# Rotary attention and two feed-forward layers on one core: weight conversion every four units, rotation and stacks as separate steps

## The chip, the cores and the metric

The kernel runs on one core of a Trainium2 chip. The metric is the device time of one execution in microseconds (us); a figure for a kernel is the median of several runs.

## The reference

The input is q, k and v for 4 batches, 8 heads, 576 positions and 64 dimensions; the output of the attention goes through two feed-forward layers of width 512 to 2048 to 512.

```python
q_rot, k_rot = (rotate(q), rotate(k))
scores = scale * np.matmul(q_rot, k_rot.transpose(0, 1, 3, 2))
attn = np.exp(scores - np.max(scores, axis=-1, keepdims=True))
attn = attn / (np.sum(attn, axis=-1, keepdims=True) + 1e-09)
x = np.matmul(attn, v)                        # to 2304 tokens x 512
h = x @ w_in                                  # first layer
g = np.where(h >= 1, h, np.where(h <= -1, 0.0, (h + 1) ** 2 / 4))
x = g @ w_out
r = np.maximum(x @ w2_in, 0.0)                # second layer
out = (s * (r * r) + b) @ w2_out
```

All matrix products are made from two float32r parts of each operand (high and low), so that one product is three matmuls: high by high, high by low, low by high. The weights come as 64-bit floats and are split into the two parts on the chip.

## The kernel before

**Attention in units.** Two heads of one batch make a pair; there are 16 pairs of nine units, 144 units in all. A unit is one block of 128 queries of one head (unit 2 of a pair: the remaining 64 of both heads). `qk` (L314) makes its scores on TensorE, the negated row maximum on VectorE (L327) and the exponent on ScalarE (L330). Two units later `tmain` and `trem` (L333, L351) transpose the result on TensorE and split it into its parts (ScalarE L345, VectorE L349); four units later `av` (L364) multiplies by v. `finish_pair` (L399) divides by the sums and writes the pair to `xd` in device memory.

**What a pair needs beforehand.** `load_qk` and `load_v` fetch q, k and v through SyncE's DMA queue. `rope_pair` (L260) rotates q or k: a multiply and an add on POOL (`pool_tt`, L83, in pieces of 288 columns), the high part on ScalarE (L270, L273), the low part on VectorE for q (L271) and on POOL for k. `stack` (L280) copies the parts to their places for the score matmuls by DMAs in SyncE's queue: `qs` for q, `kh` (high part, twice) and `kz` (low part) for k. `v_pair` (L294) splits v on ScalarE and POOL. For pair i + 1 this is written into the units of pair i: q rotated at unit 1, k at 3, v loaded at 5 and split at 7.

**Weight halves.** The first layer's weights are 16 slices, of which 8 (`set_a`) are used beside the attention: group 0 is slices 0 to 3, group 1 slices 4 to 7. Each slice has two halves (one for h, one for y), and each half is made by six steps (L106): load (SyncE, L117), `bias` (ScalarE, L127), `shift` (VectorE, L132 and L133), `high` (ScalarE, L136), `rest` (VectorE, L141 and L142) and `low_part` (POOL, L146 and L147). The scratch tiles `wa` and `wm` have one buffer, the loaded `wraw` has two, so one half follows the other. `convert(n)` (L485) takes the next half from `pending` and sets its load for unit n and its steps for n + 2, n + 2, n + 3, n + 3 and n + 4.

**Pieces.** `beside` (L435) gives the first layer's work on chunks of 288 tokens and one weight group: four h pieces and four y pieces of 12 matmuls each, 80 pieces in all, for five of the eight chunks. They go into units with a budget (`run_fill`, L501): each unit adds its share, a piece costs 1. Batch 0 feeds 16 pieces of group 0 (from unit 39 at the earliest), batch 1 feeds 48 (from unit 75), batch 2 feeds 16 (from unit 111). A new chunk is loaded and split four units ahead (`split_x`).

**Order.** The loop at L568 writes for each unit: q (scores), l (loads and preparations of the next pair), t (transposes), a (value product), f (pieces). Steps that were set for a later unit with `put` are written by `run_later` right after q; `behind` (L224) makes each of their ScalarE and VectorE instructions stand behind the last exponent and the last maximum written so far. A scheduler then fixes one order for each engine's and each DMA queue's instructions, and every engine keeps it. In the attention it may move an instruction ahead of earlier written ones where nothing ties it; instructions that are not written through `behind` (the rotation, stacks and split of v) are not tied, nor are those on POOL and SyncE.

**After the attention** the `stage` function (L593) computes the rest of the first layer and the second layer in five stages, with the other 48 weight halves converted on the way.

Of the kernel before, what the change touches and what calls it, by code (L numbers as in the profile page):

```python
# [57 lines left out]
def kernel(ctx, tc, qq, kk, vv, tab, ww1, ww2, s, b, out):  # L58
# [162 lines left out]
    def put(n, fn, *args):  # L221
        later.setdefault(n, []).append((fn, args))
# [7 lines left out]
    def run_later(n):  # L230
        for fn, args in later.pop(n, []):
            behind(fn, *args)
# [24 lines left out]
        for j in range(2):  # L257
            nc.gpsimd.memset(kz_t[j][n][D:].bitcast(F32), 0.0)

    def rope_pair(i, nm, eng, lo_eng, pieces=WHOLE):  # L260

        t = qk_in.pop((nm, i))
        hi, lo = t[:, 0, :].bitcast(F32R), t[:, 1, :].bitcast(F32R)
        for c in pieces:
            tt = pool_tt if eng is nc.gpsimd else nc.vector.tensor_tensor
            tt(out=t[:, :, c], in0=t[:, :, c], in1=tab_sb[:, :, c], op=ALU.mult)
            r = t[:, 1, c]
            tt(out=r, in0=t[:, 0, c], in1=r, op=ALU.add)
            if nm == "q":
                nc.scalar.activation(hi[:, c], r, AF.Copy, scale=0.125)  # L270
                nc.vector.scalar_tensor_tensor(out=lo[:, c], in0=r, scalar=0.125, in1=t[:, 0, c], op0=ALU.mult, op1=ALU.subtract)  # L271
            else:
                nc.scalar.copy(hi[:, c], r)  # L273
                pool_tt(out=lo[:, c], in0=r, in1=t[:, 0, c], op=ALU.subtract)
        parts_t[nm, i] = t
        if i > 0:
            stack(i, nm, 0)
            stack(i, nm, 1)

    def stack(i, nm, j):  # L280
        t = parts_t[nm, i][j * D:(j + 1) * D]
        if nm == "q":
            st = stacks["q", i, j] = qs_t[j][i % 2]
            st = st[:, j * D:j * D + S].bitcast(F32)
            nc.sync.dma_start(out=st[:D], in_=t[:, 0, :])
            return nc.sync.dma_start(out=st[D:], in_=t[:, 1, :]).ins
        kh = att.tile([P, S], F32R, tag="kh", name="kh", bufs=4)
        kz = kz_t[j][i % 2]
        stacks["k", i, j] = kh, kz
        nc.sync.dma_start(out=kh[:D].bitcast(F32), in_=t[:, 0, :])  # L290
        nc.sync.dma_start(out=kh[D:].bitcast(F32), in_=t[:, 0, :])
        return nc.sync.dma_start(out=kz[:D].bitcast(F32), in_=t[:, 1, :]).ins

    def v_pair(i):  # L294
        t = v_in[i]
        vs = att2.tile([P, 5, 4, D], F32R, tag="vs", name="vs")
        nc.scalar.copy(vs[:, :, 0::3, :], t)
        pool_tt(out=vs[:, :, 1:3, :], in0=t, in1=vs[:, :, 0::3, :], op=ALU.subtract, dim=1)
        vs_t[i] = vs

# [127 lines left out]
    def split_x(c, n):  # L428

        put(n, x_load, c)  # L430
        for k in range(KD):
            put(n + 2 + k // 2, x_split, k)
        return n + 4

    def beside(work):  # L435
        ready = split_x(work[0][0], max(now + 2, 45))
        for n, (c, gi) in enumerate(work):
            while now < ready:
                yield None
# [26 lines left out]
            load_qk(0, "k", HALVES)  # L466
    load_qk(0, "q", HALVES)
    load_v(0)
    rope_pair(0, "k", nc.vector, nc.gpsimd, HALVES)
    rope_pair(0, "q", nc.vector, nc.vector, HALVES)  # L470
    for j in range(2):
        stack(0, "k", j)
        first = stack(0, "q", j)
    v_pair(0)
    nc.sync.dma_start(out=s_sb, in_=s.to_broadcast([P, 1]))
    nc.sync.dma_start(out=b_sb, in_=b.to_broadcast([P, 1]))
    load_qk(1, "q")
# [22 lines left out]

    def run_fill(budget):  # L501
        nonlocal done
        done = min(done, 1.0)
        done += budget
        while fill and done > 0:
            try:
                cost = next(fill[0])
                if cost is None:
                    break
                done -= cost  # L510
            except StopIteration:
                fill.pop(0)
        if not fill:
            done = 0.0
# [9 lines left out]
    def do_load(n):  # L524
        if n < len(units):
            i, k = units[n]
            if i + 1 < NPAIR:
                if k == 0:
                    load_qk(i + 1, "k")
                elif k == 1:  # L530
                    rope_pair(i + 1, "q", nc.gpsimd, nc.vector)
                elif k == 3:
                    rope_pair(i + 1, "k", nc.gpsimd, nc.gpsimd)
                elif k == 5:
                    load_v(i + 1)
                elif k == 7:
                    v_pair(i + 1)
                    if i + 2 < NPAIR:
                        load_qk(i + 2, "q")

        if n in range(31, 49, 2) or n in range(70, 110, 4):
            convert(n + 1)

    def do_t(n):
        if LT <= n < len(units) + LT:
# [15 lines left out]
                    fill.append(beside(ORDERS[i // NP]))  # L561

    def do_fill(n):
        run_fill(0.0 if n < 48 else 0.85 if n < 90 else 0.98)

    acts = {"q": do_qk, "l": do_load, "t": do_t, "a": do_av, "f": do_fill}
    now = 0
    while now < len(units) + LA or fill or later:  # L568
        with ExitStack() as st:
            if now < 36:  # L570
                st.enter_context(tc.issue_after(first))
            for o in ORDER:
                acts[o](now) if now < len(units) + LA or o == "f" else None
                if o == "q":
                    run_later(now)
        now += 1
    pa.close()
    pp.close()
# [148 lines left out]
```

## Time and profile before

| | us |
|---|---|
| median of 3 runs | 1209.62 (1208.05 to 1211.63) |
| the profiled execution | 1214.03 |
| its span, first to last instruction | 1212.20 |

| | PE | VectorE (DVE) | ScalarE (ACT) | POOL |
|---|---|---|---|---|
| busy, us | 1117.4 | 789.8 | 605.1 | 608.2 |
| share of the span | 92% | 65% | 50% | 50% |

The share of a whole span mixes stages with different limits, so the argument cuts the span into stretches. PE is TensorE's matmuls, PEld its weight loads, SPq the DMA queue of SyncE. A busy PE is counted with the overlap of neighbouring matmuls, so it can be busy without being at its peak. "A <- B" in a list of waits means that A stood idle until B was done. The mean granted clock of TensorE was 0.975 of full speed.

### The profile page before, as it was taken

What the parts mean: (1) busy time and instruction counts of PE and PEld (TensorE: products, weight loads), DVE (VectorE), ACT (ScalarE), POOL (GpSimd) and SP (SyncE); (2) the same over time, 40 slices, a digit from 0 to 9 for tenths busy, and PEclk for the clock granted to TensorE, in tenths of its full rate; (3) what the DMA queues carried; (4) which work ended last, traced back from release to release, by engine and by line L of the source; (5) the groups of instructions that cost most, each with busy time, mean ns of one, the idle gap of its engine ahead of it and who ended that gap; (6) DMA issues with size and microseconds to landing.
All of it is one profiled execution on the core that took longest, in us unless ns stands there. A gap on an engine that the chain in (4) does not pass through costs nothing.

```text
span 1212.2 us, 19147 instructions
## 1 busy us (share of the span) xinstructions
PE 1117.4 (92%) x6628; PEld 1034.4 (85%) x6628; DVE 789.8 (65%) x1363; ACT 605.1 (50%) x1319; POOL 608.2 (50%) x782
## 2 busy tenths in 40 slices
PE   3898875988899999999989999999999999999998
PEld 3687764988899998999989999999888889988887
DVE  4589985789887777587766667777763333434443
ACT  3688753677677766555444443444443233222221
POOL 6778787278765401366668988566541101110100
PEclk9899877899999999999999989999999999999999
DMA  8775653365465420343335545443421101312210
GB/s 228 197 199 164 193 151 120 92 196 172 146 188 148 118 75 18 100 132 120 122 93 149 165 146 159 125 131 96 154 64 63 32 32 63 93 33 64 71 62 34
DMA packets 76033, 142.69 MB, mean 118 GB/s; under 512 B 11680, under 2 KB 49568, under 8 KB 75936
## 3 DMA queue, kind: packets, MB, share of 16 engines
q1 hardware_dynamic: 75936, 141.47, 39.5%
q8 instruction: 52, 0.85, 0.3%
q14 instruction: 45, 0.37, 0.1%
HBM read 91.29 MB, written 26.54 MB: 97 GB/s over the span
## 4 chain that ended last, share of the span: by engine, by line
PE 48%; DVE 18%; POOL 14%; issue 8%; ACT 7%; DMA 5%; SPq 1%; POOLq 0%; ACTq 0%; DVEq 0%
PE hps L154 14%; PE yps L640 5%; PE yps L642 5%; PE yps L641 5%; POOL w L83 5%; PE y L154 4%; POOL wm L83 4%; PE av L154 4%; PE sc L154 4%; PE h L154 3%; POOL xl L83 3%; PE tp L343 2%; DVE nm L327 2%; DVE wm L133 2%; ACT wa L127 2%
## 5 line engine op out<-in xcount | busy, mean ns | idle before, releaser
L154 PE MATMUL hps<-xh,w 128*128 128x464 f32 (+5 forms) x1216 | 346.6, 350 | 3.5 <-POOL w L83 2.5
L154 PEld LDWEIGHTS hps<-xh,w 128*128 128x128 f32 x1216 | 223.2, 189 | 19.1 <-POOL w L83 2.8
L640 PE MATMUL yps<-gh,w 128*128 128x464 f32 (+5 forms) x608 | 214.1, 352 | 6.8 <-ACT yo L647 5.9
L83 POOL TENSOR_TENSOR xl<-xs,xh 128x232 fp32r<-128x232 f32 (+5 forms) x140 | 107.4, 796 | 215.3 <-ACT xh L87 215.2
L641 PE MATMUL yps<-gl,w 128*128 128x464 f32 (+5 forms) x608 | 213.0, 350 | 2.5 <-DVE gl L91 2.5
L642 PE MATMUL yps<-gh,w 128*128 128x464 f32 (+5 forms) x608 | 212.5, 350 | 0.0
L154 PE MATMUL hps<-xl,w 128*128 128x464 f32 (+5 forms) x608 | 212.4, 349 | 0.0
L83 POOL TENSOR_TENSOR wm<-wm,w 128x256 f32<-128x256 f32 x128 | 114.0, 910 | 135.6 <-DVE wa L141 70.1
L327 DVE TENSOR_REDUCE nm<-sc 128x1 f32<-128x576 f32 x144 | 108.1, 751 | 47.6 <-PE sc L154 46.3
L184 DVE TENSOR_TENSOR ar<-ar,hps 128x464 f32<-128x464 f32 (+1 forms) x80 | 50.5, 632 | 132.7 <-ACT ar L183 132.7
L154 PE MATMUL sc<-kh,qs 128*128 128x288 f32 x320 | 102.3, 335 | 35.3 <-DMA qs<-qin 16.8
L640 PEld LDWEIGHTS yps<-gh,w 128*128 128x128 f32 x608 | 114.7, 189 | 18.1 <-ACT yo L647 9.2
L641 PEld LDWEIGHTS yps<-gl,w 128*128 128x128 f32 x608 | 114.9, 189 | 11.1 <-DVE gl L91 3.6
L154 PEld LDWEIGHTS hps<-xl,w 128*128 128x128 f32 x608 | 115.0, 189 | 7.6
L642 PEld LDWEIGHTS yps<-gh,w 128*128 128x128 f32 x608 | 114.8, 189 | 7.5
L330 ACT ACTIVATE p<-sc,nm 128x576 f32<-128x576 f32 x144 | 107.0, 744 | 15.0 <-DVE nm L327 10.4
L183 ACT ACTIVATE ar<-hps 128x464 f32<-128x464 f32 (+1 forms) x80 | 44.1, 553 | 124.4 <-PE hps L154 124.2
L349 DVE TENSOR_TENSOR ptl<-tp,pth 128x512 fp32r<-128x512 f32 x134 | 90.4, 682 | 22.4 <-ACT pth L345 21.8
L154 PEld LDWEIGHTS sc<-kh,qs 128*128 128x128 f32 x320 | 63.9, 200 | 45.0 <-ACT p L330 23.2
L345 ACT CAST pth<-tp 128x512 fp32r<-128x512 f32 x134 | 78.1, 586 | 46.0 <-PE tp L343 45.0
L83 POOL TENSOR_TENSOR w<-wm,wa 128x256 fp32r<-128x256 f32 x128 | 99.3, 794 | 1.4 <-DVE wa L142 1.4
L154 PE MATMUL y<-gh,w 128*128 128x288 f32 x320 | 78.1, 313 | 20.0 <-POOL w L83 11.0
(87 smaller groups left out, 2340.0 us busy)
## 6 DMA issues: line engine op xcount, KB each, us to landing
wraw<-in_ww SPq DMA_DIRECT2D x64, 512.0 KB, 3.8
kh<-kin SPq DMA_DIRECT2D x64, 144.0 KB, 2.6
qs<-qin SPq DMA_DIRECT2D x64, 144.0 KB, 2.6
qin<-in_q SPq DMA_DIRECT2D x15, 576.0 KB, 4.8
kin<-in_k SPq DMA_DIRECT2D x15, 576.0 KB, 3.9
xs<-y1d SPq DMA_DIRECT2D x32, 232.0 KB, 2.5
yd<-ys SPq DMA_DIRECT2D x40, 144.0 KB, 2.1
vin<-in_v SPq DMA_DIRECT2D x16, 320.0 KB, 3.8
```

Of the source, the lines that this page charges most:

```text
L83: nc.gpsimd.tensor_tensor(out=out[c], in0=in0[c], in1=in1[c], op=op)
L127: nc.scalar.activation(t["a"], top, AF.Copy, scale=2.0 ** -112)
L154: nc.tensor.matmul(out_ps, l, r, start=(i == 0), stop=(i == n - 1))
L183: nc.scalar.activation(r, ps, AF.Relu)
L184: nc.vector.tensor_tensor(out=r, in0=r, in1=ps, op=ALU.mult)
L327: anchors["DVE"] = nc.vector.tensor_reduce(out=nm, in_=sc[:, :, :288], axis=AX.XY, op=ALU.max, negate=True).ins
L330: anchors["ACT"] = nc.scalar.activation(p, sc[:, :, :288], AF.Exp, bias=nm, scale=1.0, accum_out=sums_t[i][:, col:col + 1]).ins
L345: nc.scalar.copy(hi, v)
L349: nc.vector.tensor_tensor(out=lo, in0=v, in1=hi, op=ALU.subtract)
L640: nc.tensor.matmul(acc, wh, gh, start=f == 0, stop=False)
L641: nc.tensor.matmul(acc, wh, gl, start=False, stop=False)
L642: nc.tensor.matmul(acc, wl, gh, start=False, stop=last)
```

## The change

- Halves: `convert` is called at units 16, 20, ..., 44 and 64, 68, ..., 92, for that unit itself. Before it was at 31, 33, ..., 47 and 70, 74, ..., 106 for the next unit (16 halves in all in both).
- Pieces: the budget starts at unit 44 (48 before) with 0.6 a unit up to 71 and 0.98 from there (0.85 up to 89, then 0.98), and up to 2.0 of it may be saved (1.0 before). The first chunk is set for now + 2; the bound "not before unit 45" is gone.
- `rope_pair`, `stack` and `v_pair` become single steps, set with `put` for the units shown below; so their ScalarE and VectorE instructions stand behind that unit's maximum and exponent. The first pair (`rope_first`) stays as it was, apart from the order of its stack DMAs.
- Loads: k of the pair after next at unit 8 and its q at unit 6 (k of the next pair at 0, q of the pair after next at 7 before); v at 2 (5 before).
- `run_later` moves from behind q to the end of the unit.

```diff
-    def rope_pair(i, nm, eng, lo_eng, pieces=WHOLE):
...
+    def rope_mult(i, nm):
+        t = parts_t[nm, i] = qk_in.pop((nm, i))
+        pool_tt(out=t, in0=t, in1=tab_sb, op=ALU.mult)
+
+    def rope_add(i, nm):
+        t = parts_t[nm, i]
+        pool_tt(out=t[:, 1, :], in0=t[:, 0, :], in1=t[:, 1, :], op=ALU.add)
+
+    def rope_hi(i, nm):
...
+    def rope_lo(i, nm):
...
+    def stack_q(i):
...
+    def stack_k(i):
+        for j in range(2):
+            t = parts_t["k", i][j * D:(j + 1) * D]
+            kh = att.tile([P, S], F32R, tag="kh", name="kh", bufs=4)
+            stacks["k", i, j] = kh, kz_t[j][i % 2]
+            nc.sync.dma_start(out=kh[:D].bitcast(F32), in_=t[:, 0, :])
+            nc.sync.dma_start(out=kh[D:].bitcast(F32), in_=t[:, 0, :])
+
+    def stack_z(i):
+        for j in range(2):
+            t = parts_t["k", i][j * D:(j + 1) * D]
+            nc.sync.dma_start(out=kz_t[j][i % 2][:D].bitcast(F32), in_=t[:, 1, :])
...
-        ready = split_x(work[0][0], max(now + 2, 45))
+        ready = split_x(work[0][0], now + 2)
...
-        done = min(done, 1.0)
+        done = min(done, 2.0)
...
                 if k == 0:
-                    load_qk(i + 1, "k")
-                elif k == 1:
-                    rope_pair(i + 1, "q", nc.gpsimd, nc.vector)
-                elif k == 3:
-                    rope_pair(i + 1, "k", nc.gpsimd, nc.gpsimd)
-                elif k == 5:
-                    load_v(i + 1)
-                elif k == 7:
-                    v_pair(i + 1)
-                    if i + 2 < NPAIR:
-                        load_qk(i + 2, "q")
-
-        if n in range(31, 49, 2) or n in range(70, 110, 4):
-            convert(n + 1)
+                    if i == 0:
+                        load_qk(1, "k")
+                    for dn, fn, nm in ((0, rope_mult, "q"), (1, rope_add, "q"), (2, rope_hi, "q"), (3, rope_lo, "q"),
+                                       (2, rope_mult, "k"), (3, rope_add, "k"), (4, rope_hi, "k"), (5, rope_lo, "k")):
+                        put(n + dn, fn, i + 1, nm)
+                    put(n + 2, load_v, i + 1)
+                    put(n + 4, stack_q, i + 1)
+                    put(n + 5, stack_k, i + 1)
+                    put(n + 6, stack_z, i + 1)
+                    put(n + 5, v_hi, i + 1)
+                    put(n + 6, v_lo, i + 1)
+                if k == 6 and i + 2 < NPAIR:
+                    load_qk(i + 2, "q")
+                if k == 8 and i + 2 < NPAIR:
+                    load_qk(i + 2, "k")
+
+        if n in range(16, 48, 4) or n in range(64, 96, 4):
+            convert(n)
...
-        run_fill(0.0 if n < 48 else 0.85 if n < 90 else 0.98)
+        run_fill(0.0 if n < 44 else 0.6 if n < 72 else 0.98)
...
             for o in ORDER:
                 acts[o](now) if now < len(units) + LA or o == "f" else None
-                if o == "q":
-                    run_later(now)
+            run_later(now)
```

## Rows read from the trace of the kernel before

**Rows 1.** windows: start:end, length, busy us (x instructions) of each engine, clock, DMA
```profile
65.20:137.00 71.80, 62.25 (x430) 54.94 (x429) 66.81 (x115) 57.40 (x135) 54.21 (x74) 0.95 0.67 187
137.00:247.30 110.30, 82.52 (x518) 75.90 (x518) 80.16 (x137) 63.64 (x148) 67.32 (x84) 0.85 0.45 130
247.30:267.90 20.60, 17.69 (x136) 16.39 (x134) 19.64 (x37) 17.38 (x43) 16.76 (x21) 1.00 0.67 203
267.90:338.10 70.20, 62.98 (x449) 59.37 (x450) 62.67 (x114) 50.03 (x120) 54.34 (x66) 0.98 0.57 163
338.10:507.40 169.30, 162.55 (x1233) 157.63 (x1232) 125.54 (x245) 115.98 (x286) 61.25 (x79) 1.00 0.36 104
```

**Rows 2.** the same view, units 36 to 53
```profile
103.80:151.00 47.20, 37.97 (x256) 33.39 (x253) 45.48 (x77) 36.55 (x85) 35.88 (x48) 0.93 0.69 192
```

**Rows 3.** waits of the engines, 137.0 to 247.3 us: total, times, longest
```profile
PE y L154 <- POOL w L83: 11.0, 3, 8.8
...
ACT kin L273 <- POOL kin L83: 8.0, 1, 8.0
```

**Rows 4.** waits of SyncE's DMA queue, the same stretch
```profile
SPq L117 <- DVE wa L142: 23.4, 5, 8.5
```

**Rows 5.** groups by line, whole span: busy us, mean ns, idle before
```profile
L142 DVE SCALAR_TENSOR_TENSOR wa<-wraw,wa 128x512 f32<-128x512 uint16 x64 | 58.9, 920 | 1.1
...
L83 POOL TENSOR_TENSOR kin<-kin 128x288 fp32r<-128x288 f32 (+1 forms) x62 | 53.1, 871 | 7.7 <-ACT kin L273 7.7
...
L133 DVE SCALAR_TENSOR_TENSOR wm<-wa,wm 128x512 uint32<-128x512 uint32 x64 | 50.1, 783 | 0.8
...
L136 ACT CAST w<-wm 128x512 fp32r<-128x512 f32 x64 | 39.8, 621 | 35.3 <-DVE wm L133 34.4
...
L132 DVE TENSOR_SCALAR wm<-wa 128x512 uint32<-128x512 uint32 x64 | 35.8, 559 | 61.6 <-ACT wa L127 61.4
...
L141 DVE TENSOR_SCALAR wa<-wm 128x512 uint32<-128x512 uint32 x64 | 32.2, 503 | 0.8
```

**Rows 6.** chain that ended last, 223 to 233 us: start, us, what
```profile
224.15 1.32 PE av L154 x9
...
227.06 0.53 PE sc L154 x4
227.59 0.44 PE tp L343 x4
228.02 1.59 PE h L154 x12
```

**Rows 7.** windows of the h pieces
```profile
338.10:507.40 169.30, 41.47 (x276) 37.72 (x276) 20.59 (x47) 1.00 0.36 104
```

**Rows 8.** windows of the y pieces
```profile
338.10:507.40 169.30, 45.69 (x287) 39.83 (x288) 8.66 (x22) 1.00 0.36 104
```

**Rows 9.** windows of L127, the first step of a half
```profile
65.20:137.00 71.80, 2.01 (x3) 0.95 0.67 187
...
267.90:338.10 70.20, 4.04 (x6) 0.98 0.57 163
```

**Rows 10.** instructions of L142 and of L349: ns min/median/max
```profile
L142 DVE SCALAR_TENSOR_TENSOR wa<-wraw,wa x64: 673/937/1286, 110.9 to 889.1; 128x512 f32<-128x512 uint16 x64
...
L349 DVE TENSOR_TENSOR ptl<-tp,pth x134: 620/681/693, 30.5 to 494.5; 128x512 fp32r<-128x512 f32 x134
```

**Rows 11.** DMA issues of L292 (kz): who waited for them, time to landing
```profile
  PEld sc L154: 1.7, 1
...
DMA to landing us min/median/max: 2.3/2.7/5.7
```

**Rows 12.** SyncE's queue around 85 us: start, us
```profile
84.95 0.46 SPq L292 DMA_DIRECT2D kz<-kin  x1
```

**Rows 13.** TensorE around 181 us: start, us
```profile
181.41 0.44 PE L154 MATMUL sc<-kz,qs 128*128 128x288 f32 x1
181.65 0.44 PE L154 MATMUL sc<-kh,qs 128*128 128x288 f32 x1
```

More of the change, by code (lines that the diff above doesn't have):

```diff
@@ L258, with rope_first @@
             nc.gpsimd.memset(kz_t[j][n][D:].bitcast(F32), 0.0)
-    def rope_pair(i, nm, eng, lo_eng, pieces=WHOLE):
-        t = qk_in.pop((nm, i))
+    def rope_first(nm):
+        t = parts_t[nm, 0] = qk_in.pop((nm, 0))
         hi, lo = t[:, 0, :].bitcast(F32R), t[:, 1, :].bitcast(F32R)
-        for c in pieces:
-            tt = pool_tt if eng is nc.gpsimd else nc.vector.tensor_tensor
-            tt(out=t[:, :, c], in0=t[:, :, c], in1=tab_sb[:, :, c], op=ALU.mult)
+        for c in HALVES:
+            nc.vector.tensor_tensor(out=t[:, :, c], in0=t[:, :, c], in1=tab_sb[:, :, c], op=ALU.mult)
             r = t[:, 1, c]
-            tt(out=r, in0=t[:, 0, c], in1=r, op=ALU.add)
+            nc.vector.tensor_tensor(out=r, in0=t[:, 0, c], in1=r, op=ALU.add)
             if nm == "q":
@@ L273, in rope_pair @@
                 nc.scalar.copy(hi[:, c], r)
[L274 to L281, printed above, removed]
-        if nm == "q":
-            st = stacks["q", i, j] = qs_t[j][i % 2]
-            st = st[:, j * D:j * D + S].bitcast(F32)
-            nc.sync.dma_start(out=st[:D], in_=t[:, 0, :])
[L286 to L299, printed above, removed]
+                nc.gpsimd.tensor_tensor(out=lo[:, c], in0=r, in1=t[:, 0, c], op=ALU.subtract)
+    def rope_mult(i, nm):
[4 more added lines that the diff above has]
+        pool_tt(out=t[:, 1, :], in0=t[:, 0, :], in1=t[:, 1, :], op=ALU.add)
@@ new lines, in rope_hi @@
+    def rope_hi(i, nm):
+        t = parts_t[nm, i]
+        hi = t[:, 0, :].bitcast(F32R)
+        if nm == "q":
+            nc.scalar.activation(hi, t[:, 1, :], AF.Copy, scale=0.125)
+        else:
+            nc.scalar.copy(hi, t[:, 1, :])
+    def rope_lo(i, nm):
+        t = parts_t[nm, i]
+        lo, r = t[:, 1, :].bitcast(F32R), t[:, 1, :]
+        if nm == "q":
+            nc.vector.scalar_tensor_tensor(out=lo, in0=r, scalar=0.125, in1=t[:, 0, :], op0=ALU.mult, op1=ALU.subtract)
+        else:
+            pool_tt(out=lo, in0=r, in1=t[:, 0, :], op=ALU.subtract)
@@ new lines, in stack_q @@
+    def stack_q(i):
+        for j in range(2):
+            t = parts_t["q", i][j * D:(j + 1) * D]
+            stacks["q", i, j] = qs_t[j][i % 2]
+            st = qs_t[j][i % 2][:, j * D:j * D + S].bitcast(F32)
+            nc.sync.dma_start(out=st[:D], in_=t[:, 0, :])
+            first = nc.sync.dma_start(out=st[D:], in_=t[:, 1, :])
+        return first.ins
+    def stack_k(i):
[5 more added lines that the diff above has]
+            nc.sync.dma_start(out=kh[D:].bitcast(F32), in_=t[:, 0, :])
@@ L303, with v_hi, v_lo @@
+    def stack_z(i):
+        for j in range(2):
+            t = parts_t["k", i][j * D:(j + 1) * D]
+            nc.sync.dma_start(out=kz_t[j][i % 2][:D].bitcast(F32), in_=t[:, 1, :])
+    def v_hi(i):
+        vs_t[i] = att2.tile([P, 5, 4, D], F32R, tag="vs", name="vs")
+        nc.scalar.copy(vs_t[i][:, :, 0::3, :], v_in[i])
+    def v_lo(i):
+        vs = vs_t[i]
+        pool_tt(out=vs[:, :, 1:3, :], in0=v_in[i], in1=vs[:, :, 0::3, :], op=ALU.subtract, dim=1)
     UNITS = [(0, 2), (0, 3), (None, 4), (0, 0), (0, 1), (1, 0), (1, 1), (1, 2), (1, 3)]
@@ L468 @@
     load_v(0)
[L469 to L474, printed above, removed]
+    rope_first("k")
+    rope_first("q")
+    stack_k(0)
+    stack_z(0)
+    first = stack_q(0)
+    v_hi(0)
+    v_lo(0)
     nc.sync.dma_start(out=s_sb, in_=s.to_broadcast([P, 1]))
```

## Prediction

> **What bounds the kernel now.** I read the busy slices of the page first: they split the span into the attention with pieces of the first feed-forward in its gaps (to 507 us) and the feed-forward stages after it. The change touches only the first. So I cut that part at units: a unit is one query block of one head pair, and it can be seen as one max-reduce on VectorE (L327). Unit 18 starts at 65.2 us, 48 at 137.0, 72 at 247.3, 81 at 267.9, 99 at 338.1, and the last piece ends near 507.4. Rows 1 give the engines in these stretches, and they have different limits:
> - Units 18 to 47 (71.8 us): VectorE, 66.81 us busy, 93%. In the denser half of it and a little beyond it is 45.48 of 47.2, 96.4% [rows 2]. TensorE only follows.
> - Units 48 to 71 (110.3 us, with 16 pieces): no engine is the limit. TensorE's clock is 0.85 and VectorE falls to 73%. This is the stall that can be removed. The waits name it: matmuls of the y pieces stood 11.0 us for the low parts of the weights on POOL, and ScalarE stood 8.0 us at one rotation cast for POOL [rows 3]. SyncE's own queue stood 23.4 us in 5 weight loads, whose buffer was still being read [rows 4]. All three are one pile-up: the halves come every two units, one set of scratch buffers makes them go one after the other, and loads, rotations and casts behind them in the in-order queues wait too.
> - Units 81 to 98: 62.98 of TensorE and 62.67 of VectorE in 70.2 us, both near their limit. From unit 99 TensorE alone is (162.55 of 169.3) [rows 1].
>
> **Prices.** One weight half costs VectorE 0.559 + 0.783 + 0.503 + 0.920 = 2.77 us [rows 5]. On TensorE, back to back, a piece is 12 matmuls in 1.59 us; four score matmuls take 0.53, four transposes 0.44, nine of the value product up to 1.32 [rows 6]. A pair of nine units has 40 score matmuls (5.3), 50 transposes (5.5) and four value products (5.3): 16.1 us, 1.79 a unit. The last stretch has units 99 to 143, 45 of them, and (276 + 287)/12 = 47 pieces [rows 7, 8]: 80.6 + 74.7 = 155.3 us at least, and it took 169.3, that is 1.09 times that. Where both engines are near their limit, units 81 to 98 with 17 pieces (32.2 + 27.0 = 59.2 of TensorE, 62.67 of VectorE) took 70.2, 1.12 times the larger.
>
> **The change, part by part.**
> 1. *Halves at units 16, 20, ..., 44 and 64, 68, ..., 92.* Before, three halves had begun by unit 48 and two and a half were done [rows 9]; now 7.5 would be. Five more halves in units 18 to 47: VectorE 66.81 + 13.85 = 80.7 us, at 96.4% busy 83.7: **+12 us**. With the slack used up entirely it is +9. Row and rule differ here. The last VectorE step of a half (L142) lasts from 673 to 1286 ns, while the split of the transposes (L349), which reads one operand from PSUM, stays within 620 and 693 [rows 10]. The Trainium skill (SBUF — State Buffer, Who interferes with whom) says that a VectorE instruction with two SBUF inputs and a POOL instruction that reads SBUF shut each other out for a whole instruction. The trace agrees as far as these two rows go; by that rule, POOL being fuller now, L133 and L142 would sit at their long ends, and this term would be about +18 instead of +12 and the time 1194.6, an estimate from the rows' maxima. I keep the mean and put the long end into the range.
> 2. *Pieces from unit 44, at 0.6 a unit to unit 71.* Following the loop by hand, the first x chunk is loaded at 46 and the first piece comes at unit 50 instead of 54; the 16 pieces of group 0 end at 71 instead of 70. All 8 halves that they need are planned to end by unit 48, the first y piece is at 53. Without the pile-up units 48 to 71 cost TensorE 24 x 1.79 + 16 x 1.59 = 68.4 us, times 1.09 74.6. VectorE loses four of the 6.5 halves it had here: 80.16 - 11.1 = 69.1, times 1.12 77.4. I take 77 against 110.3: **-33 us**. Bounds: -38 if only TensorE binds, and -20 if part of the pile-up stays.
> 3. *Units 72 to 80, without pieces in both.* One half more: VectorE 19.64 + 2.77 = 22.4, over 0.964 23.2 instead of 20.6: **+3 us**.
> 4. *Units 81 to 98.* Four halves instead of six [rows 9], 5.5 us of VectorE less, but the same pieces for TensorE: between 0 and -6, I take **-3 us**.
> 5. *From unit 99*: the pieces end at unit 146 instead of 150, but TensorE has the same matmuls: 0, between -3 and +3. The stages from 507.4 on start from the same state: 0.
> 6. *Rotation, stacks and split of v as steps.* The same instructions per pair, so nothing in busy time. Each ScalarE and VectorE step now stands behind the exp and the max-reduce of its unit; queued behind a step that waits are that engine's later exps and reduces. With the cast two units behind its multiply, the wait of the 8.0 us kind should be rare; its gain is already inside part 2. SyncE's queue is passed in another order: v is loaded at 2 instead of 5, the next k at 8 of the pair before instead of 0, and the stacks stand at 4, 5 and 6 instead of 1 and 3. What hides the later stacks is the turns of units 7 and 8; rival A prices the loss of that cover. In units 0 to 17 the step places hardly matter, as the first loads set them: -4 to +4, taken as 0.
>
> Sum: +12 - 33 + 3 - 3 = **-21 us**. The profiled execution took 1214.03 us, 4.4 above the median of 1209.62, and 1.8 of it lie outside the span. The difference carries over: 1193 for such an execution, **1188.6** for the median.
>
> **Rivals.**
> - *A, slower: the stacks come too late.* The next pair's first score matmuls need kz. Its chain now begins at the end of unit 4: ScalarE's cast, POOL's two subtracts (2 x 0.871 [rows 5]), six SyncE issues of 0.46 [rows 12] (2.8), then 2.7 to 5.7 to land [rows 11]: 7.8 to 10.8 us with a cast of some 0.6 (L136's 0.621 has the shape nearest to it [rows 5]). Four turns of 2.8 us (units 5 to 8) less the one by which TensorE runs ahead leave 8.4. Today kz is hardly waited for (1.7 us in all [rows 11]), but it is also early: for the pair that starts at 103.8 it was issued at 84.95 [rows 12]. From a mean of 21/15 = 1.4 us at each of 15 pair starts the gain is gone. At the middle, 9.3 - 8.4 and 1.5 for other work ahead of it on POOL (an estimate, about two of its instructions), 2.4 us, it costs 36: **1225**. Against it: in units 48 to 98 a turn is 3.2 us or more. Chance 0.14.
> - *B, the halves still come late.* With one every four units, units 81 to 98 took 70.2/6 = 11.7 us a half [rows 9], about the planned four units. But each has five steps on three engines, and each step now stands behind a turn. From 67 us on, eight at 15 us would end near 187; the first y piece is due near 162, so TensorE would stand some 25 us, of which the first stretch, with fewer halves in it, gives back 4: **1210**, no difference. Chance 0.12.
> - *C, the clock.* In units 18 to 47 TensorE would be needed for 30 x 1.79 = 53.7 of 84 us, 64%. In the 18 units where it was needed for 32.2 of 47.2 us, 68%, the granted clock was 0.93 [rows 2]. At the lower level, 1.2 GHz, score matmuls start 0.24 us apart instead of 0.13 [rows 6, 13]. If the whole stretch ran so, 53.7 would become some 97, 13 more than 84: **1202**; this alone would still leave a gain. The 0.93 says that it bites rarely. Chance 0.05. The Trainium skill (TensorE: Matmul & The Clock Gate, What's actually happening) has the throttled clock as the default that activity releases, which speaks for this rival; the trace agrees in so far as the clock was 0.85 in the stall [rows 1].
>
> **How the numbers follow.** Forecast 0.69, A 0.14, B 0.12, C 0.05. The forecast alone runs from 1175 to 1203: the bounds of part 2 (-5, +13) and the long end of part 1 (+6) with the small terms. A and B lie above, so for 8 in 10 the range goes to 1214 at the top; below it goes to 1172, in case the steps free more than I count. About 0.3%, 3.6 us, is what a measurement can tell from no change. Faster: the forecast, C, and a sixth of B, 0.76; same: most of B, 0.10; slower: A, 0.14.
>
> **What would show it.** Unit 48 starts near 149 us (137.0 before) and unit 72 near 226 (247.3). The wait of y matmuls for POOL's w falls from 11 us to under 3, that of the weight loads on SyncE from 23 to under 5, and VectorE is 95% busy in units 18 to 47. Wrong: unit 48 later than 155 (the steps are dearer), gaps at each pair start with kz or kh as releaser (A), y pieces that still wait for w (B), a clock under 0.8 in units 18 to 47 (C).

## The result, and the profile after

The changed kernel takes 1221.86 us (median of 4 runs, 1221.03 to 1225.29) beside 1208.84 for the kernel before: ratio 1.010, 95% interval 1.007 to 1.013. It is slower by 13 us where 21 less were forecast, and it lies above the range. The profiled execution took 1225.29 us with a span of 1223.5; it is the slowest of the four.

Cut at the same units, the windows of the changed kernel are these: start:end, length, busy us (x instructions) of PE, PEld, VectorE, ScalarE and POOL, then TensorE's clock and the DMA's share and GB/s. The first line is units 0 to 17, the others are units 18 to 47, 48 to 71, 72 to 80, 81 to 98, 99 to the last piece, and what follows it.

```profile
19.30:61.10 41.80, 38.04 (x224) 30.87 (x223) 23.07 (x36) 29.45 (x70) 25.82 (x35) 0.96 0.66 195
61.10:143.90 82.80, 65.11 (x424) 58.36 (x423) 73.06 (x126) 58.76 (x138) 66.57 (x85) 0.90 0.60 168
143.90:228.10 84.20, 72.76 (x512) 68.21 (x511) 70.30 (x125) 59.20 (x141) 58.30 (x74) 0.94 0.54 146
228.10:253.80 25.70, 20.79 (x146) 19.19 (x146) 23.10 (x42) 19.53 (x46) 17.61 (x23) 0.93 0.79 218
253.80:330.20 76.40, 66.08 (x457) 61.38 (x455) 59.02 (x109) 48.01 (x116) 54.63 (x69) 0.96 0.49 145
330.20:506.60 176.40, 162.83 (x1214) 154.60 (x1213) 127.28 (x242) 114.55 (x284) 59.87 (x78) 1.00 0.35 103
506.60:1223.50 716.90, 695.45 (x3662) 643.22 (x3660) 409.03 (x676) 268.63 (x525) 309.62 (x396) 0.98 0.31 96
```

Beside [rows 1]: units 48 to 71 fell from 110.3 to 84.2, as they should. Unit 72 starts at 228.1 instead of 247.3, and the forecast said 226. Of these 19 us all is given back and more: +5 in units 72 to 80, +6 in 81 to 98, +7 from unit 99, where the forecast had +3, -3 and 0, and +12 behind the last piece (716.9 against 704.5), where the forecast had nothing.

The stall's own waits went or shrank. Of [rows 3] neither wait is in the list any more (the y matmuls' for POOL's w, ScalarE's for POOL), and of the 23.4 us of [rows 4] about half is left in units 48 to 71 (SyncE's queue; us in total, times, longest):

```profile
SPq L117 <- DVE wa L142: 12.7, 3, 12.1
```

### The profile page after: what moved, and what is told of

The parts are those of the page before. It is cut to its first block, busy times and chain, and to the rows that moved or that the text cites. A ratio compares the mean times of both kernels' runs of the same rounds, so it can differ in the third digit from the quotient of the medians.

```text
span 1223.5 us, 19142 instructions
## 1 busy us (share of the span) xinstructions
PE 1122.3 (92%) x6628; PEld 1037.1 (85%) x6628; DVE 792.0 (65%) x1363; ACT 601.8 (49%) x1319; POOL 604.5 (49%) x782
## 4 chain that ended last, share of the span: by engine, by line
PE 51%; DVE 15%; POOL 13%; issue 7%; DMA 7%; ACT 6%; SPq 1%; POOLq 0%; DVEq 0%; ACTq 0%
PE hps L154 17%; PE yps L673 6%; PE yps L674 6%; PE yps L672 6%; PE sc L154 4%; PE av L154 4%; POOL w L83 4%; POOL wm L83 3%; PE y L154 3%; PE h L154 3%; POOL xl L83 3%; DMA kz<-kin 3%; PE tp L371 2%; DVE wm L133 2%; DVE nm L355 2%
## 5 line engine op out<-in xcount | busy, mean ns | idle before, releaser
L154 PE MATMUL hps<-xh,w 128*128 128x464 f32 (+5 forms) x1216 | 348.6, 352 | 2.8 <-ACT xh L87 2.8
L154 PEld LDWEIGHTS hps<-xh,w 128*128 128x128 f32 x1216 | 225.4, 191 | 18.4 <-ACT xh L87 3.4
L154 PE MATMUL hps<-xl,w 128*128 128x464 f32 (+5 forms) x608 | 214.1, 352 | 1.1 <-POOL xl L83 1.1
L154 PE MATMUL sc<-kh,qs 128*128 128x288 f32 x320 | 103.1, 337 | 34.6 <-DMA qs<-qin 18.1
L154 PEld LDWEIGHTS hps<-xl,w 128*128 128x128 f32 x608 | 116.1, 191 | 9.6 <-POOL xl L83 2.0
L358 ACT ACTIVATE p<-sc,nm 128x576 f32<-128x576 f32 x144 | 107.2, 745 | 18.8 <-DVE nm L355 12.9
L377 DVE TENSOR_TENSOR ptl<-tp,pth 128x512 fp32r<-128x512 f32 x134 | 90.6, 682 | 24.2 <-ACT pth L373 23.4
L183 ACT ACTIVATE ar<-hps 128x464 f32<-128x464 f32 (+1 forms) x80 | 44.2, 553 | 124.9 <-PE hps L154 124.6
L154 PEld LDWEIGHTS sc<-kh,qs 128*128 128x128 f32 x320 | 64.9, 203 | 42.9 <-ACT p L358 23.0
L371 PE MATMUL tp<-ident,p 128*128 128x128 f32 x576 | 91.8, 285 | 10.0 <-DVE ptl L377 9.7
```

Of the source, the lines that this page charges most:

```text
L154: nc.tensor.matmul(out_ps, l, r, start=(i == 0), stop=(i == n - 1))
L183: nc.scalar.activation(r, ps, AF.Relu)
L358: anchors["ACT"] = nc.scalar.activation(p, sc[:, :, :288], AF.Exp, bias=nm, scale=1.0, accum_out=sums_t[i][:, col:col + 1]).ins
L371: nc.tensor.transpose(v[:, c, :], p_t[i, k][:, c * P:(c + 1) * P], ident)
L377: nc.vector.tensor_tensor(out=lo, in0=v, in1=hi, op=ALU.subtract)
```

## Where it went: the stages

Behind the attention the first stage needs x, which SyncE's queue loads (xs). The queue at the end of the attention, start, us, what, first in the kernel before (xs is L609), then in the changed one (xs is L641):

```profile
482.81 6.07 SPq L459 DMA_DIRECT2D yd<-ys  x4
495.27 0.80 SPq L609 DMA_DIRECT2D xs<-xd  x2
```

```profile
483.99 23.35 SPq L487 DMA_DIRECT2D yd<-ys  x5
507.44 0.87 SPq L641 DMA_DIRECT2D xs<-xd  x2
```

Before, four pieces stood behind the attention's last matmul, and the x loads went out at 495 beside them. Now the pieces end with the attention. The store of a y piece waits in SyncE's queue for ScalarE's copy of it, and the loads stand behind that store until 507.4. The wait (480 to 515 us: total, times, longest), and TensorE behind it (the attention's last matmul, then the stage's first):

```profile
SPq L487 <- ACT ys L486: 23.8, 4, 17.5
```

```profile
507.87 0.27 PE L436 MATMUL rr<-ident,sume 128*128 128x128 f32 x1
510.29 0.40 PE L154 MATMUL hps<-xh,w 128*128 128x288 f32 x1 [2.15 <-ACT xh L87]
```

So the stage starts 3.7 us after the last piece (506.5), and for 2.15 us of these TensorE has nothing to do. Then its clock falls. Windows of the changed kernel, and the same place in the one before:

```profile
511.00:521.20 10.20, 8.75 (x32) 7.72 (x33) 3.10 (x6) 4.44 (x11) 8.30 (x12) 0.50 0.65 182
506.60:565.00 58.40, 53.73 (x368) 51.90 (x367) 38.73 (x77) 28.54 (x65) 35.90 (x43) 0.91 0.43 126
```

```profile
504.00:565.00 61.00, 60.62 (x456) 59.99 (x454) 42.62 (x83) 32.83 (x75) 41.27 (x50) 1.00 0.46 138
```

For 10.2 us the granted clock was 0.50, the 1.2 GHz level, with only 32 matmuls in it; before it stayed at 1.00. The Trainium skill (TensorE: Matmul & The Clock Gate, What's actually happening) has the throttled clock as the default that activity releases; these rows agree in so far as the clock fell behind the idle 2.15 us.

## The experiments

All times are medians in us, each with its ratio to the kernel before on the same chip. The kernel before had medians of 1208.8 to 1211.8 us in these comparisons, so rows of different chips are compared with some 3 us of room. The stretches are of the profiled execution alone, from the first unit's maximum (17 to 21 us into the span), cut at units 48, 72, 99 and the end of the last piece. W are the halves, F the pieces' budget (start, share, saved budget), R the rotation, stacks and split of v as steps, L the later `run_later`; the change is W+F+R+L. "Hold" writes no pieces in units 126 to 129; "POOL order" and "untied" are explained where they come.

| kernel | us | ratio, 95% interval | 0-47 | 48-71 | 72-98 | 99-piece | stages |
|---|---|---|---|---|---|---|---|
| before | 1208.84 | | 119.0 | 110.3 | 90.8 | 169.5 | 704.5 |
| after | 1221.86 | 1.010 (1.007 to 1.013) | 124.6 | 84.2 | 102.1 | 176.2 | 717.0 |
| e1 after + hold | 1214.79 | 1.004 (1.001 to 1.007) | 121.6 | 84.4 | 105.9 | 175.8 | 705.5 |
| e2 W+F+L | 1212.16 | 1.000 (0.998 to 1.003) | 120.4 | 97.5 | 94.4 | 165.1 | 712.4 |
| e3 R+L | 1235.29 | 1.019 (1.013 to 1.024) | 116.4 | 107.2 | 99.0 | 184.1 | 705.4 |
| e4 after, 1.0 saved | 1212.49 | 1.001 (0.998 to 1.004) | 122.7 | 81.1 | 100.0 | 177.4 | 708.6 |
| e5 L | 1210.48 | 1.001 (0.999 to 1.003) | 118.1 | 108.9 | 87.8 | 171.9 | 704.8 |
| e6 W | 1199.14 | 0.992 (0.989 to 0.995) | 120.6 | 86.7 | 92.4 | 172.2 | 704.9 |
| e7 W+F+L, hold | 1207.74 | 0.997 (0.995 to 0.999) | 125.4 | 96.1 | 95.7 | 167.6 | 705.3 |
| e8 W+F, hold | 1207.48 | 0.998 (0.995 to 1.000) | 120.3 | 99.0 | 100.0 | 166.6 | 704.9 |
| e9 R+L, POOL order | 1228.47 | 1.013 (1.010 to 1.016) | 114.2 | 109.8 | 99.2 | 181.4 | 704.0 |
| e10 after, POOL order | 1210.19 | 1.000 (0.998 to 1.002) | 121.7 | 78.8 | 105.5 | 169.1 | 712.1 |
| e11 W+R+L, POOL order | 1209.57 | 0.999 (0.996 to 1.001) | 124.2 | 83.8 | 94.2 | 179.8 | 705.3 |
| e12 W+F+L, 1.0 saved | 1209.17 | 0.998 (0.996 to 1.000) | 121.9 | 93.5 | 97.8 | 168.1 | 708.8 |
| e13 after, POOL order, hold, 1.0 saved | 1217.60 | 1.005 (1.001 to 1.008) | 121.3 | 81.1 | 108.2 | 175.0 | 704.3 |
| e14 as e11, untied | 1197.64 | 0.990 (0.986 to 0.993) | 119.0 | 81.7 | 92.7 | 179.9 | 704.3 |
| e15 after, POOL order, untied | 1213.40 | 1.001 (0.997 to 1.005) | 117.3 | 84.9 | 106.1 | 178.6 | 712.6 |
| e16 W+R+L | 1224.61 | 1.010 (1.007 to 1.014) | 126.7 | 89.7 | 95.2 | 186.6 | 704.5 |

A stretch is no exact measure. On every engine e1 runs in the same order as the changed kernel until 440 us, and e7 in the same order as e2 until 432 us; still their stretches before that differ by up to 3.8 us (72 to 98) and 5.0 us (0 to 47). The profiled execution is one run: in e13 it was among the fastest (1210.8, median 1217.6), in e15 the slowest (1221.8, median 1213.4).

**The end of the pieces (e1).**

```diff
     def do_fill(n):
+        if 126 <= n < 130:
+            return
         run_fill(0.0 if n < 44 else 0.6 if n < 72 else 0.98)
```

> The changed kernel with one thing more: no pieces are written in units 126 to 129, so the last 20 pieces come up to four units later and end at unit 150 as before the change, instead of 146; four of them stand behind the last unit again. In the changed kernel the stages behind the attention take 716.9 us instead of 704.8. Theory T (lost cover): the last pieces used to run while the first stage's x was loaded and split; now they end with the attention, TensorE stands idle for 3.7 us, its clock falls for 10.2 us and the stages start late. Then the stretch behind the last piece falls by 8 to 12 us and the kernel to 1210 to 1216. Rival (the stages are slower for another reason, the order of conversions and stores in them): it stays within 3 us of 1222. What TensorE does inside the attention is the same work in both theories, so the end of the last piece should be within 3 us of 506.6.

The x loads go out at 495.53, TensorE has no pause before the stage's first matmul, and the stages take 705.5 instead of 717.0; the medians differ by 7 us. The lost cover is shown, and the other rows bear it out. Where no piece begins behind the attention's last matmul (the changed kernel, e2, e10, e15), the stages take 712.1 to 717.0; with two pieces behind it (e4, e12) 708.6 and 708.8; with four or more, in the other twelve, 704.0 to 705.5. What is left above the kernel before lies in the attention.

**The rotation (e2, e3, e5).** e2 is the change without its steps, so against the change:

```diff
-                    for dn, fn, nm in ((0, rope_mult, "q"), (1, rope_add, "q"), (2, rope_hi, "q"), (3, rope_lo, "q"),
...
+                elif k == 1:
+                    rope_pair(i + 1, "q", nc.gpsimd, nc.vector)
+                elif k == 3:
+                    rope_pair(i + 1, "k", nc.gpsimd, nc.gpsimd)
...
```

e3 is the kernel before with the steps and the moved `run_later`, e5 with that move alone:

```diff
             for o in ORDER:
                 acts[o](now) if now < len(units) + LA or o == "f" else None
-                if o == "q":
-                    run_later(now)
+            run_later(now)
```

> The changed kernel with the rotation, stacks and split of v as in the kernel before: one block each at units 1, 3 and 7, v loaded at 5, not tied behind a maximum or exponent. Halves, pieces and the place of the later steps stay as changed. Theory T: the pairs with pieces from unit 81 on (9 to 12, some 12 us slower than before the change with about the same pieces) are slow because of the rotation steps, so the stretch from unit 81 to the last piece falls by 10 us or more. Rival B (bursts: up to three pieces in one unit, since 2.0 of the budget may be saved): they stay as slow, as the bursts are still in. Rival A (late stacks): waits of score matmuls for kz and kh, 8.2 us in the changed kernel, go below 3. The tail stays uncovered, so the time is 1208 to 1214 by T and 1218 to 1222 by the rival.

> The kernel before with the rotation steps alone (and later steps at the end of the unit, without which they can't be placed): halves still at 31 to 47 and 70 on, pieces still from unit 48. Theory T: the stall in units 48 to 71 stays in its greater part, since the halves are what it waits for (110 us before, over 95 here), and the pairs 9 to 12 get slower by some 10 us: 1210 to 1225. Rival (the pile-up was one of rotation steps in ScalarE's and POOL's queues, so freeing them is what helps): units 48 to 71 fall under 92 us, and the kernel to 1190 to 1200.

> The kernel before with one thing changed: the steps set for a later unit (halves, loads and splits of x) are written at the end of their unit instead of right behind its scores. The rotation alone came to 1235 us, but it needs this too. Theory T (the rotation steps themselves cost): this edit alone stays within 5 us of 1209.5. Rival L (the later place of the steps costs: h pieces stood 7.5 us for POOL's split of x in the rotation run): 1217 to 1230, with waits of h pieces for xl of 4 us or more behind unit 99.

Moving `run_later` costs nothing that can be measured. The steps by themselves cost some 24 us, most of them behind unit 99 (184.1 against 169.5), and leave the stall where it was (107.2). So they are not what removes it, and they aren't neutral either. Taken out of the change they are worth 10: from unit 81 to the last piece e2 takes 236 us where the change takes 253. Beside the new budget they do shorten units 48 to 71 (84.2 with them, 97.5 without), which the rest of the attention more than takes back.

**The halves alone (e6).**

```diff
-        if n in range(31, 49, 2) or n in range(70, 110, 4):
+        if n in range(15, 47, 4) or n in range(63, 95, 4):
             convert(n + 1)
```

So the halves are set for the same units as in the change, from one unit earlier, as `run_later` still stands behind q.

> The kernel before with the weight halves alone at units 16, 20, ..., 44 and 64, ..., 92; rotation, pieces and everything else as before. Theory T (the halves were what the stall in units 48 to 71 waited for): units 18 to 47 grow from 71.8 to some 80 to 84 us, units 48 to 71 fall from 110.3 to 80 to 90, the tail is covered as before, and the kernel comes to 1188 to 1202. Rival (the stall needs the thinner pieces too): units 48 to 71 stay over 95 and the kernel over 1203.

Faster than both kernels. Its windows, units 18 to 47 and 48 to 71, and those of L127, the first step of a half, in the same stretches:

```profile
63.10:138.90 75.80, 61.78 (x429) 52.74 (x428) 70.38 (x124) 60.04 (x138) 59.06 (x76) 1.00 0.72 190
138.90:225.60 86.70, 72.60 (x502) 64.94 (x502) 71.50 (x129) 59.17 (x140) 62.88 (x81) 0.98 0.53 148
...
63.10:138.90 75.80, 3.36 (x5) 1.00 0.72 190
138.90:225.60 86.70, 3.37 (x5) 0.98 0.53 148
```

The stall is gone with this edit alone (86.7), and the extra halves cost units 18 to 47 only 4 us, which is within what two executions differ by: five begin there, not seven or eight, and VectorE stays at 93%. The clock goes with it: between unit 18 and the last piece the trace has TensorE at 0.50 for 10.2 us in e6, 44.4 before and 37.5 in the change. Whether this is a part of the gain or follows from it no run tells.

**The budget (e4, e7, e8, e12).** e4 is the change with this:

```diff
-        done = min(done, 2.0)
+        done = min(done, 1.0)
```

e7 is e2 with the hold of e1. e8 is e7 with `run_later` behind q and the halves set from the unit before. e12 is the kernel before with the halves, the moved `run_later` and this, so e2 with the saved budget of before:

```diff
-            ready = split_x(work[0][0], max(now + 2, 45))
+            ready = split_x(work[0][0], now + 2)
...
-        run_fill(0.0 if n < 48 else 0.85 if n < 90 else 0.98)
+        run_fill(0.0 if n < 44 else 0.6 if n < 72 else 0.98)
```

> The changed kernel with the saved budget bounded by 1.0 as before, so at most two pieces come in one unit instead of three. Rival B (bursts): value products stood 6.0 us for VectorE's maximum step of the h pieces, ten times, and score matmuls for the first x; without bursts the stretch from unit 81 to the last piece falls by 6 us or more, to 1212 to 1216. Theory T: it stays within 3 us of 1222. The pieces end at unit 146 to 147, so the tail is the same.

> The changed kernel with the old rotation (1212 us with the last piece at 494.9 and 712.4 us of stages behind it) and with no pieces written in units 126 to 129, so that the last four stand behind the last unit. Theory T (lost cover): the stages behind the last piece go back to 704 to 707 us while the last piece ends at 495 to 499: 1201 to 1206. Rival (the cover only moves the loss into the attention): 1209 to 1213.

> The same as the run with the old rotation and the late last pieces, but the steps set for a later unit are written right behind its scores, as before the change; halves still at 16, 20, ..., 44 and 64, ..., 92, pieces at 0.6 and 0.98. Rival L (the later place costs): 4 to 8 us less than that run, 1194 to 1201. Theory T: within 3 us of it.

> The kernel before with the halves every four units and the pieces' new start and shares (from unit 44, 0.6 and then 0.98), but with at most 1.0 of the budget saved as before; rotation as before. If the share and the early start cost the 10 us that units 48 to 71 lost beside the new budget (97.5 with it, 86.7 with the halves alone): units 48 to 71 95 to 99 us, 1206 to 1213 in all. If the saved budget of 2.0 did (pieces in bursts): units 48 to 71 at most 89 us, 1197 to 1203 in all.

e7's stages come back as e1's did (705.3 against 712.4), but the kernel gains only 4 us on e2, and 1207.7 lies between its two cases; its profile has 5 us more in units 0 to 47 than e2's, where the two kernels are the same. e8 is the same as e7, so the place of `run_later` costs nothing here either.

Beside the old rotation, start and share alone take back 10 of the 12 us that the halves bring (1209.2 against 1199.1): in the profiles 7 in units 48 to 71, 5 in 72 to 98 and 4 in the stages, while from unit 99 they give back 4. e12's units 48 to 71:

```profile
139.20:232.70 93.50, 75.10 (x479) 67.28 (x479) 74.20 (x127) 58.56 (x138) 63.34 (x81) 0.91 0.49 135
```

There are fewer matmuls in it than in e6's line (479 against 502), it is 7 us longer, and the clock is 0.91 instead of 0.98. The lower share thins out the matmuls that TensorE had; whether the clock is cause or consequence no run tells.

The saved budget of 2.0 costs 9 us in the change (e4), and 3 that can hardly be measured beside the old rotation (e2, e12). But e4's expectation had the place wrong: from unit 81 to the last piece it takes 250 us, only 3 less than the change, and the stages 708.6 instead of 717.0. With 1.0 saved two pieces come behind the attention's last matmul again. So most of these 9 us are the cover once more, and not bursts.

**What in the steps costs (e9 to e11, e16).** In the changed kernel POOL does this in units 77 to 79 (kin without tab_sb, as fp32r, are the low parts of k; kin with tab_sb is the multiply). The second block is SyncE's queue:

```profile
242.63 1.56 POOL L83 TENSOR_TENSOR kin<-kin 128x288 fp32r<-128x288 f32 x2 [1.00 <-ACT kin L289]
247.23 1.55 POOL L83 TENSOR_TENSOR kin<-kin,tab_sb 128x288 f32<-128x288 f32 x2 [3.04 <-DVE wa L141]
```

```profile
242.27 0.34 SPq L241 DMA_DIRECT2D kin<-in_k  x1
...
245.81 1.18 SPq L319 DMA_DIRECT2D kz<-kin  x2
```

The low part of the present k has been copied to kz when a k is multiplied again, before unit 81 begins a new pair: it is the *next* pair's k, whose multiply is set for unit 83. Nothing tied POOL and SyncE, so the load and the multiply had been moved ahead as far as a buffer allowed. In e16 it can be seen what that costs. POOL, then SyncE's queue, then the waits from unit 99 on in e16 (POOL and TensorE) and in the changed kernel (POOL):

```profile
339.81 0.81 POOL L424 COPY eb<-sume 128x512 f32<-128x512 f32 x1
357.54 3.09 POOL L83 TENSOR_TENSOR kin<-kin,tab_sb 128x288 f32<-128x288 f32 x4 [16.92 <-DMA xd<-u]
360.59 3.11 POOL L83 TENSOR_TENSOR kin<-kin 128x288 f32<-128x288 f32 x4
363.64 1.82 POOL L83 TENSOR_TENSOR vs<-vin,vs 128x128 fp32r<-128x128 f32 x3
365.42 3.06 POOL L83 TENSOR_TENSOR xl<-xl,xh 128x288 fp32r<-128x288 f32 x4
```

```profile
347.18 0.38 SPq L450 DMA_DIRECT2D xl<-xd  x1
347.66 1.10 SPq L305 DMA_DIRECT2D qs<-qin  x2
353.15 0.33 SPq L241 DMA_DIRECT2D kin<-in_k  x1
```

```profile
POOL kin L83 <- DMA xd<-u: 49.0, 3, 16.9
...
PE h L154 <- POOL xl L83: 6.3, 3, 2.5
```

```profile
POOL kin L83 <- DMA xd<-u: 15.2, 1, 15.2
```

The multiply at 357.5 is set for unit 110 and comes in unit 104. Its load goes out only when q's copies have left a buffer free; POOL stands 16.9 us for it (the list names a store, but the load was issued 4.4 us before the multiply began, and such loads land 4.0 us after their issue, the page's median). The low parts of the present k, of v and of x (xl, loaded at 347) stand behind it in POOL's order, and h pieces wait for xl.

So e9, e10 and e11 tie POOL: the multiply of q behind the split of v of the pair before, that of k behind the add of q.

```diff
     def rope_mult(i, nm):
         t = parts_t[nm, i] = qk_in.pop((nm, i))
-        pool_tt(out=t, in0=t, in1=tab_sb, op=ALU.mult)
+        with ExitStack() as st:
+            if prior:
+                st.enter_context(tc.issue_after(prior[-1]))
+            pool_tt(out=t, in0=t, in1=tab_sb, op=ALU.mult)
```

> The kernel before with the rotation, stacks and split of v as steps (as in the run of these alone, 1235.3 us) and one thing more: on POOL the multiply of q stands behind the split of v of the pair before, and the multiply of k behind the add of q, so that POOL cannot take up a pair before it has done with the one ahead of it. Theory POOL order (in the steps, POOL's multiply of the next pair's k was placed a pair early, ahead of the low parts of the present k and of x, and stood waiting for a load): 1210 to 1222 us, the stretch from unit 99 to the last piece falls from 184 to 170 to 176, POOL's waits of 40.3 us in 3 for a load there to under 20, and the h pieces' waits for xl on POOL (16 us with the weight loads) to under 4. Rival, the turns (ScalarE's and VectorE's steps behind their unit cost it, POOL's order is harmless): 1230 to 1238, the stretch 181 or more.

> The changed kernel with the same order on POOL. POOL order: the attention is 8 to 12 us shorter, mostly behind unit 72, last piece at 495 to 499 us, and since the end of the pieces still meets the end of the attention the stages stay over 709: 1208 to 1216 us. The turns: last piece at 504 or later, 1218 to 1226.

> The kernel before with the halves every four units (1199.1 us alone), the steps, and the order on POOL; the pieces' budget as before. POOL order: 1197 to 1206 us, and under 1199 only if the steps free something once POOL is in order. The turns: 1215 to 1223, the halves' 1199 and most of the 24 that the steps cost by themselves.

> The changed kernel with the pieces' budget as before (from unit 48, 0.85 and 0.98, at most 1.0 saved). If the budget costs beside the steps what it cost beside the old rotation (10 to 13 us): 1209 to 1213, stages behind the last piece 704 to 707. If POOL's order and the tie of the steps already are the limit and hide it: 1216 to 1224.

POOL's wait for the load is gone in e9 to e11. The order was worth 12 us in the change (1221.9 to 1210.2), 15 beside the halves (1224.6 to 1209.6) and 7 for the steps alone, where 13 or more were expected (1228.5 lies just under the rival's range, the turns). The 1209.6 of e11 lies between its two cases: something else costs another 10 us there. How POOL's order comes to 12 and 15 us is seen only in part: from unit 99 on TensorE's waits for xl were 6.3 us in e16 and 2.1 in the change, and are gone in e11 and e10.

e16 came out just above its second case. With the steps in, the new budget costs nothing in all: the profile of the change has 12 us more in the stages and 7 more in units 72 to 98 than e16's, and 16 less in units 48 to 71 and from unit 99.

**The tie to the unit (e14, e15).** e14 is e11, and e15 is e10, with the steps written plainly in their units:

```diff
         for fn, args in later.pop(n, []):
-            behind(fn, *args)
+            if fn in (rope_mult, rope_add, rope_hi, rope_lo, stack_q, stack_k, stack_z, load_v, v_hi, v_lo):
+                fn(*args)
+            else:
+                behind(fn, *args)
```

> The kernel of halves, steps and the order on POOL (1209.6 us, against 1199.1 with the halves alone), but the steps of the rotation, the stacks and the split of v no longer stand behind their unit's maximum and exponent. If it is that tie on ScalarE and VectorE that costs the remaining 10 us: 1197 to 1203, units 18 to 47 at most 79 us (85.5 with the tie, 75.8 with the halves alone). If it is the places of the steps and of the stacks' DMAs: 1206 to 1213, units 18 to 47 over 82.

> The changed kernel with the order on POOL kept (1210.2 us so) and its rotation, stacks and split of v no longer tied behind the unit. If the tie costs 10 us in the change as it does beside the halves alone: 1198 to 1204. If the pieces' new budget takes that gain, because they end with the attention and leave the stages uncovered (over 709 us behind the last piece): 1206 to 1212.

Beside the halves the tie is worth 12 us. The low part of k comes late with it. The score matmuls' waits for kz in e11, then in e14 (L155 is L154 of the other kernels; the weight loads' line and the matmuls' line count mostly the same time):

```profile
PEld sc L155 <- DMA kz<-kin: 10.7, 6, 4.1
PE sc L155 <- DMA kz<-kin: 9.1, 4, 3.9
```

```profile
PEld sc L155 <- DMA kz<-kin: 1.7, 1, 1.7
PE sc L155 <- DMA kz<-kin: 1.5, 1, 1.5
```

Units 18 to 47, first of e14, then of e11, have TensorE and VectorE 3 and 5 us busier in 11 us more. Six of these are a shift, as e11 is through units 0 to 17 that much sooner; up to unit 48 the tie costs 5 us:

```profile
65.00:139.40 74.40, 63.78 (x427) 56.10 (x426) 70.14 (x126) 60.40 (x139) 62.54 (x77) 0.93 0.66 185
```

```profile
58.60:144.10 85.50, 67.21 (x425) 59.38 (x424) 75.31 (x128) 59.76 (x137) 62.03 (x80) 0.88 0.60 165
```

In e15, beside the new budget, the gain isn't there: 1213.4, with runs from 1205.6 to 1221.8, above both of its cases.

**Everything mended (e13)**: e10 with the hold and 1.0 saved.

> The changed kernel with all three losses mended at once: POOL's order kept (as in the run that gave 1210.2), no pieces written in units 126 to 129 so that the last four follow the attention (as in the run that gave 1214.8), and at most 1.0 of the budget saved (1212.5). If the three causes are separate places and add up, with the tail counted once: 1221.9 - 11.7 - 7 to 10 = 1200 to 1204 us, stages behind the last piece 704 to 707. If they are one cause seen three times (any small shift of the order gives back about 10 us): 1207 to 1214.

1217.6, with runs from 1209.4 to 1223.1, above both of its cases, so the losses don't add up. The profile is of a run of 1210.8 and can't show where the median's 7 us more lie. In it the stages take 704.3, but even there TensorE stands once behind the last piece (504.6), and the clock was 0.66 from 507 to 512:

```profile
506.76 0.40 PE L682 MATMUL yps<-gh,w 128*128 128x288 f32 x1 [2.21 <-ACT ys L494]
```

Units 72 to 98 take 108.2. What the new budget does in units 72 to 98 beside the steps (100 to 108 us in the six such kernels, 93 to 99 in the five with the steps and the budget of before) stays open.

## Why the prediction was wrong

1. *Halves, units 18 to 47, +12 (part 1).* Measured +11, but not for the reason given. About 5 of it are a shift: units 0 to 17 took 41.8 us instead of 47.1, and up to unit 48 the change costs 5.6. The price of a half held roughly (2.96 us instead of 2.77); their number didn't. Rival B's objection applies: five steps, each behind a turn, so 5 or 6 halves began there instead of 7.5 done, and VectorE had 73.06 us of work instead of 80.7, 88% of the stretch. The windows of L127, L133 and L142 in that stretch, one view each:

```profile
61.10:143.90 82.80, 4.07 (x6) 0.90 0.60 168
...
61.10:143.90 82.80, 3.57 (x5) 0.90 0.60 168
...
61.10:143.90 82.80, 4.86 (x5) 0.90 0.60 168
```

   e6 puts the halves' own cost at 4; the rest goes with the tie (85.5 with it in e11, 74.4 without in e14). What the prediction drew from the Trainium skill's port rule (SBUF — State Buffer, Who interferes with whom), that L133 and L142 would sit at their long ends, did not come: their means here were 0.71 us (3.57 in 5) and 0.97 (4.86 in 5), against a mean of 0.783 and a longest L142 of 1.286 before [rows 5, 10], with POOL busy for 80% of the stretch.
2. *The stall, -33 (part 2).* Right in place and cause, a little large: -26 in the change, -24 with the halves alone. The new share and start, which stand in the same part, do not help: without the steps they leave 97.5 (e2). Its bound of -38 should be -36, by its own 74.6.
3. *Units 72 to 98: +3 and -3 (parts 3 and 4).* Measured +5 and +6. The four halves instead of six did not come, as the halves run late: L127 starts six times in units 81 to 98, as before. "But the same pieces for TensorE" was wrong in small (19 pieces begin in units 81 to 98, 17 before; two pieces are 3.2 us). Without bursts of saved budget, which had no price, it is still 100.0 (e4). The cause of the rest stays open.
4. *The stages, 0 (part 5).* This is the step that failed most: +12. Its "the pieces end at unit 146 instead of 150, but TensorE has the same matmuls" counts work and overlooks order: the last four pieces were the cover for the next stage's loads (e1, e7). The prediction asked what hides the stacks, and for the loads behind the attention it did not. The +7 from unit 99, in the same part, goes when POOL's order is kept (169.1 in e10), so it belongs to the next point.
5. *The steps, 0 (part 6).* The second failure: alone they cost 24 us. No busy time came with them, as said, but waits did. One was foreseen as rival A, the late kz, in the right place, but priced far too high: 6.4 us of waits in the whole changed kernel, not 36:

```profile
PEld sc L154 <- DMA kz<-kin: 6.4, 5, 2.0
```

   The other, POOL taking up a pair too early, was not foreseen; the prediction named SyncE's new order, but not POOL's. Keeping POOL's order gave 12 us in the change and 15 beside the halves (e10, e11), untying the steps another 12 beside the halves (e14).

The forecast's place for the gain was right, and its number was far off because two terms that it put at nothing cost 12 us and more each. Of the signs named ahead, unit 72 near 226 (it was 228) and the end of the w wait came. VectorE's 95% did not (88%), nor did SyncE's wait for weight loads fall under 5 us (12.7), and unit 48 came at 143.9 instead of 149. A kernel with the halves alone (1199.1), or with untied steps and POOL in order as well (1197.6, the same within the intervals), beats both.

## What to carry to other kernels

Work that runs past the end of a stage may be the cover for the next stage's loads: before ending it earlier, look at what is issued beside it and what stands ahead of those loads in their queue. When steps are split up and some are tied to a place, the untied ones move too, as far ahead as their buffers allow, and an in-order engine then waits for something that nobody needs yet. A change of several parts is best measured part by part: here one line had the whole gain, and the costs of the others hid one another. And when an edit gives back time, look in which stretch: the saved budget's 9 us lay in the stages, not where the pieces stand.

## What the runs showed of the hardware

A short pause of TensorE between two stages cost more than itself here. In the rows above 456 matmuls took 61.0 us before, 0.134 each; by that the 368 of the changed kernel take 49.2 of its 58.4 us, and 9.2 are lost. Of these about 4.3 are idle time (58.40 - 53.73 = 4.7 us, 0.4 before), of which the pause is 2.15 and waits for the first parts of x most of the rest. The other 4.9 are slower matmuls, and the 10.2 us at a clock of 0.50 behind the pause are the place for them. In the three other kernels whose pieces end with the attention (e2, e10, e15) TensorE paused for 2.2 us as well, and its clock was then 0.50 for 6.8 us.
